# Reordering the first loads of a linear-attention and GeGLU kernel: key weights moved between two DMA queues, keys of a third tile filled in

## The chip, the cores and the metric

One core of one Trainium2 chip. The metric is the device time of one execution, in microseconds; smaller is better. The span in the profile runs from the first to the last instruction, about 1.3 us less than that time.

In the profile lines PE is TensorE, DVE VectorE, ACT ScalarE, and SPq SyncE issuing loads. L341 is line 341 of the kernel, the plain loads; L353 are the transposing loads, L453 and L454 key products, L468 and L469 query products, L539 (L541 in the changed kernel) joint products. A line of a timeline gives start, duration, engine, line and shape; the bracket at its end is the idle time before it and what ended it.

## The reference, cut to what matters

With x of 2048 x 640 in bf16, the result is `g * a + (1 - g) * b`: a linear-attention block `a` (32 heads of 20), a gated feed-forward block `b`, and a gate `g` per row.

```python
def _A_ref(x, wqkv, wo):
    qkv = (x @ wqkv) ...                     # q, k, v
    phi = lambda t: jnp.where(t > 0, t + 1, jnp.exp(t)) + 1e-6
    pq, pk = phi(q), phi(k)
    kv, z = pk^T v, sum(pk)
    return (pq kv / pq z) @ wo               # (per head; written short)

x = A_x
g = sigmoid((x * gate_w).sum(-1))
b = (gelu(x @ w_gate) * (x @ w_up)) @ w_down
```

The change touches only the start: the products of the first four row tiles of x with the key and the query weights.

## The kernel before: the parts concerned

The 640 rows of the key weights `wk` and of the query weights `wq` are cut into five chunks of 128; "wk 2" is chunk 2. A tile is 128 rows of x. Tile 0 is loaded plainly and transposed on TensorE; tiles 1 to 15 are transposed by the DMA. Each load has its own semaphore. "sp" is SyncE's queue, "act" ScalarE's.

```python
load_x(0)
load_wk(0)
load_xT(1)
load_wk(3)
load_wk(4)
load_wk(1, "act")
load_wk(2, "act")
...                                   # gate_w on "act"
for i in range(2, NQ):                # NQ = 4
    load_xT(i)
for k in range(KC):                   # KC = 5
    load_wq(k)
for i in range(NQ, NT):
    load_xT(i)
```

`KM(n, ks)` multiplies chunks `ks` of the keys of tile n (512 and 128 columns, two matmuls a chunk), `QM` the queries (the 129th column is the gate). The products of a tile with the keys, or with the queries, are one job. Job n uses two of the eight PSUM banks (where TensorE puts its results), `slot(n) = SLOTS[n % 4]`, so a query of tile 0 waits until ScalarE and VectorE (`phi1`, `phi2`) have read the keys of tile 0, and so on.

```python
for k in range(3):
    KM(0, [k])
for k in range(3):
    KM(1, [k])
KM(0, [3])
KM(1, [3])
gate_col()
KM(0, [4])
KM(1, [4])
for n in range(2 * NQ):
    if n in (2, 3):
        KM(n, ALLK)
    if n == NQ:
        for k in ALLK:
            QM(NQ, [k])               # tile 0 and tile 1 alternate
            QM(NQ + 1, [k])
    if n > NQ + 1:
        QM(n, ALLK)
    phi1(n)
    phi2(n)
for i in range(NQ, NT):
    KQ(i)                             # keys and queries of a tile together
```

Of the kernel before, what the change touches and what calls it, by code (L numbers as in the profile page):

```python
# [24 lines left out]
NQ = 4  # L25
# [137 lines left out]
def bass_gated_mix__linear_attn_block__geglu_ffn__prompt_kernel(  # L163
# [63 lines left out]
    with (  # L227
# [8 lines left out]
        with contextlib.ExitStack() as stack:  # L236
# [12 lines left out]
            def new_dma_key():  # L249
                k = "in%d" % dma_next[0]  # L250
                dma_next[0] += 1
                return k
# [16 lines left out]
            wk = wkq[:, :, 0:640]  # L269
# [38 lines left out]
            r_xT = [P.sb("xT%d" % i, R_XT, R_XT + KC * S) for i in range(NT)]  # L308
            r_xTa = [P.sb("xTa%d" % i, R_XT, R_XT + S) for i in range(NXN)]
            r_wk = [P.sb("wk%d" % k, R_WK + k * WW, R_WK + k * WW + 640) for k in range(KC)]  # L310
# [29 lines left out]
            def dma_in(dst, src, writes, reads=(), eng="sp"):  # L340
                P.op(eng, lambda e, dst=dst, src=src: e.dma_start(dst, src),  # L341
                     reads=reads, writes=writes, dma=new_dma_key())
# [3 lines left out]
            def load_x(i, eng="sp"):  # L346
                dma_in(x_aug[:, i, 0:640], A_x[0, i * 128:(i + 1) * 128, :], [r_xn[i]], eng=eng)

            def load_wk(k, eng="sp", after=()):
                dma_in(wk[:, k, :], A_wqkv[k * 128:(k + 1) * 128, 640:1280], [r_wk[k]], reads=after, eng=eng)  # L350

            def load_xT(i, after=()):
                P.op("sp", lambda e: e.dma_start_transpose(xT[:, :, i * 128:(i + 1) * 128],  # L353
                                                           A_x[0, i * 128:(i + 1) * 128, :]),
                     reads=list(after), writes=[r_xT[i]], dma=new_dma_key())

            def load_wq(k, eng="sp"):
                dma_in(wq[:, k, 0:640], A_wqkv[k * 128:(k + 1) * 128, 0:640], [r_wq[k]], eng=eng)
# [3 lines left out]
                 writes=[P.res("touch")], dma=new_dma_key())  # L362
            load_x(0)
            load_wk(0)
            load_xT(1)
            load_wk(3)
            load_wk(4)
            load_wk(1, "act")
            load_wk(2, "act")

            zero = nc.const_aps.tensor(0.0, (128, 1), F32)
            P.op("act", lambda e: e.activation(eg[:, 0:1], zero, ACT.Exp), writes=[r_eg[0]])
            P.op("dve", lambda e: e.memset(gw_sb, 0.0), writes=[r_gw])
            dma_in(gw_sb[0:5, :], gate_w.rearrange("(k p) -> k p", p=128), [r_gw], eng="act")
            for i in range(2, NQ):
                load_xT(i)
            for k in range(KC):
                load_wq(k)
            for i in range(NQ, NT):
                load_xT(i)  # L380
# [7 lines left out]
            for c in range(NHC):  # L388
# [9 lines left out]
                 reads=[r_ones], writes=[r_ident])  # L398
# [16 lines left out]
            def warm(count, n):  # L415
                def fn(e):
                    last = None
                    for w in range(count):
                        last = e.matmul(ps[:, 4, 0:n], one_l, one_r[:, 0:n], start=True, stop=True)
                    return last  # L420
                P.op("pe", fn, writes=[bank[4]])
# [4 lines left out]
            def slot(n):  # L426
                return SLOTS[n % 4]
# [17 lines left out]
            def KM(n, ks):  # L445
                i = seq[n][1]
                b0, b1 = slot(n)

                def fn(e):
                    last = None  # L450
                    for k in ks:
                        lhs = xT[:, k, i * 128:(i + 1) * 128]
                        e.matmul(ps[:, b0, :], lhs, wk[:, k, 0:512], start=(k == 0), stop=(k == KC - 1))  # L453
                        last = e.matmul(ps[:, b1, 0:128], lhs, wk[:, k, 512:640],  # L454
                                        start=(k == 0), stop=(k == KC - 1))
                    return last
                P.op("pe", fn, reads=[r_xTa[i] if i < NXN and ks == [0] else r_xT[i]] + [r_wk[k] for k in ks],
                     writes=[bank[b0], bank[b1]])

            def QM(n, ks):  # L460
                i = seq[n][1]
                b0, b1 = slot(n)

                def fn(e):
                    last = None
                    for k in ks:
                        lhs = xT[:, k, i * 128:(i + 1) * 128]
                        e.matmul(ps[:, b0, :], lhs, wq[:, k, 0:512], start=(k == 0), stop=(k == KC - 1))  # L468
                        last = e.matmul(ps[:, b1, 0:129], lhs, wq[:, k, 512:641],  # L469
                                        start=(k == 0), stop=(k == KC - 1))  # L470
                    return last
                P.op("pe", fn, reads=[r_xT[i], r_gcol] + [r_wq[k] for k in ks],
                     writes=[bank[b0], bank[b1]])

            def phi1(n):
                b0, b1 = slot(n)
                m = n % 4
                P.op("act", lambda e: e.activation(e_buf[m], ps_flat[:, b0 * 512:b0 * 512 + 640], ACT.Exp),
                     reads=[bank[b0], bank[b1]], writes=[r_e[m]])
                kind, i = seq[n]  # L480
                if kind == "q":
                    P.op("act", lambda e: e.activation(eg[:, i:i + 1], ps[:, b1, 128:129], ACT.Tanh, scale=0.5),
                         reads=[bank[b1]], writes=[r_eg[i]])

            def phi2(n):
                b0, b1 = slot(n)
                m = n % 4
                P.op("dve", lambda e: e.tensor_scalar(e_buf[m], e_buf[m], 1.0, EPS, ALU.min, ALU.add),
                     reads=[r_e[m]], writes=[r_e[m]])
                kind, i = seq[n]  # L490
                dst, r_dst = (pk[i], r_pk[i]) if kind == "k" else (pq[i], r_pq[i])
                P.op("dve", lambda e: e.scalar_tensor_tensor(
                    dst, ps_flat[:, b0 * 512:b0 * 512 + 640], 1.0 + EPS, e_buf[m], ALU.add, ALU.max),
                    reads=[bank[b0], bank[b1], r_e[m]], writes=[r_dst])

            def gate_col():

                P.op("pe", lambda e: e.matmul(ps[:, 7, 0:5], gw_sb, ident[:, 0:5], start=True, stop=True),
                     reads=[r_gw, r_ident], writes=[bank[7]])
                P.op("dve", lambda e: e.tensor_copy(wq[:, :, 640:641], ps[:, 7, 0:5].unsqueeze(2)),  # L500
                     reads=[bank[7]], writes=[r_gcol])
# [4 lines left out]
            T(0, [0], 7)  # L506
            T(0, [1, 2, 3, 4], 6)
            warm(2, 128)
            for k in range(3):
                KM(0, [k])  # L510
            for k in range(3):
                KM(1, [k])
            KM(0, [3])
            KM(1, [3])
            gate_col()
            KM(0, [4])
            KM(1, [4])
            ALLK = list(range(KC))
            for n in range(2 * NQ):
                if n in (2, 3):  # L520
                    KM(n, ALLK)
                if n == NQ:
                    for k in ALLK:
                        QM(NQ, [k])
                        QM(NQ + 1, [k])
                if n > NQ + 1:
                    QM(n, ALLK)
                phi1(n)
                phi2(n)
# [36 lines left out]
            for i in range(NQ, NT):  # L566
                KQ(i)
                if i == 4:
                    late_constants()
            P.op("dve", lambda e: e.tensor_scalar(gg, eg, 0.5, 0.5, ALU.mult, ALU.add),  # L570
                 reads=r_eg, writes=[r_g])
            P.op("dve", lambda e: e.tensor_scalar(omg, eg, -0.5, 0.5, ALU.mult, ALU.add),
                 reads=r_eg, writes=[r_omg])
# [7 lines left out]
                 reads=[r_omg], writes=[r_od], dma=new_dma_key())  # L581
# [44 lines left out]
            def ME(g):  # L626
# [6 lines left out]
                for c in cs:  # L633
# [8 lines left out]
                 reads=r_pk[0:2], writes=[r_tmp[0]])  # L642
            for i in range(2, NT):
                P.op("dve", lambda e, i=i: e.tensor_tensor(zacc, zacc, pk[i], ALU.add),  # L644
                     reads=[r_tmp[0], r_pk[i]], writes=[r_tmp[0]])
# [283 lines left out]
```

## Time and profile before

| | before |
|---|---|
| time, median of 6 runs | 273.81 us (273.72 to 274.07) |
| span | 272.6 us, PE busy 98% |
| first key product | 4.45 us |
| keys of tile 2 | 8.12 us, PE waited 0.58 us for its transpose |
| first query | 10.85 us |
| first joint product (first matmul of `KQ`) | 16.30 us |

The lines behind the table are in the prediction. The last row is the yardstick of this document. From the first joint product on PE works without a stop worth naming, and the device time less that moment is 257.6 to 257.7 us in all profiled kernels here (273.97 - 16.30 = 257.67 before). So whatever this change does shows up in that one moment.

### The profile page before, as it was taken

Reading aid. Unit: us, or ns where it says so; the run is one execution under the profiler, and the core shown is the slowest. Engines: PE = TensorE matmul, PEld = TensorE weight load, DVE = VectorE, ACT = ScalarE, POOL = GpSimd, SP = SyncE. Lnnn points to the kernel's source line nnn. Section 1 sums busy time; section 2 is a strip of 40 time slices with the busy share of each in tenths; the row PEclk is TensorE's granted clock in tenths of the full one; section 3 lists DMA queues with packets and bytes.
Section 4 is the critical chain, followed back from the end, with each engine's and each line's share of the span. In section 5 each row is a group of like instructions: output and inputs, shape, how many; then the busy total and the mean of one; then the engine's idle time right before and its main releaser. Section 6 shows DMA issues by size and latency. Waiting matters only on the chain.

```text
span 272.6 us, 3416 instructions
## 1 busy us (share of the span) xinstructions
PE 267.6 (98%) x1341; PEld 127.9 (47%) x1367; DVE 140.8 (52%) x247; ACT 75.9 (28%) x132; POOL 30.0 (11%) x28
## 2 busy tenths in 40 slices
PE   8999999999999999999999999999999999999997
PEld 3555555544445454444444444444444444444444
DVE  1678989997233335999999999634210000000200
ACT  2455555210422453232222233224011122121021
POOL 5000000003240002242332422000000000000000
DMA  7976999600200011514121221273031110110211
GB/s 192 202 115 127 346 399 388 140 2 19 58 19 2 23 50 51 192 34 49 26 48 25 49 48 27 60 219 105 5 77 38 41 38 19 38 41 19 58 58 41
DMA packets 42864, 23.78 MB, mean 87 GB/s; under 512 B 32223, under 2 KB 41439, under 8 KB 42719
## 3 DMA queue, kind: packets, MB, share of 16 engines
q1 hardware_dynamic: 42517, 23.22, 31.9%
q10 hardware_dynamic: 330, 0.33, 0.3%
q8 instruction: 11, 0.18, 0.3%
q14 instruction: 6, 0.05, 0.1%
HBM read 13.83 MB, written 2.63 MB: 60 GB/s over the span
## 4 chain that ended last, share of the span: by engine, by line
PE 96%; DMA 1%; SPq 1%; issue 1%; DVE 0%
PE ps L700 41%; PE ps L864 23%; PE ps L539 12%; PE ps L596 6%; PE ps L843 4%; PE ps L468 2%; PE ps L811 2%; PE ps L678 2%; PE ps L599 1%; DMA pool<-in_A_x_dram 1%; PE ps L453 1%; PE ps L824 1%; SPq L341 1%; PE ps L721 1%; SPq L353 0%
## 5 line engine op out<-in xcount | busy, mean ns | idle before, releaser
L700 PE MATMUL ps<-pool 128*128 128x512 bf16 x510 | 113.0, 379 | 0.5
L700 PEld LDWEIGHTS ps<-pool 128*128 128x128 bf16 x520 | 50.5, 98 | 60.0
L864 PE MATMUL ps<-pool 128*128 128x512 bf16 (+2 forms) x300 | 62.4, 366 | 0.3
L706 ACT ACTIVATE pool<-ps 128x512 f32<-128x512 f32 x52 | 31.0, 597 | 73.1 <-PE ps L700 73.1
L708 DVE TENSOR_TENSOR pool<-ps,pool 128x512 bf16<-128x512 f32 x52 | 34.7, 689 | 31.7 <-PE ps L700 30.4
L864 PEld LDWEIGHTS ps<-pool 128*128 128x128 bf16 x306 | 29.2, 98 | 33.4 <-issue 0.4
L847 DVE TENSOR_TENSOR pool<-ps,pool 128x512 bf16<-128x512 f32 x4 | 2.8, 690 | 61.5 <-PE ps L843 61.5
L539 PE MATMUL ps<-pool 128*128 128x512 bf16 (+1 forms) x176 | 32.5, 343 | 0.2
L754 POOL TENSOR_TENSOR pool<-pool 128x640 f32<-128x640 bf16 x16 | 22.4, 1404 | 73.0 <-DVE pool L756 65.6
L871 ACT ACTIVATE pool<-ps,pool 128x512 bf16<-128x512 f32 (+1 forms) x16 | 10.9, 680 | 68.6 <-PE ps L864 68.6
L539 PEld LDWEIGHTS ps<-pool 128*128 128x128 bf16 x180 | 17.6, 98 | 15.0
L558 DVE SCALAR_TENSOR_TENSOR pool<-ps,pool 128x128 bf16<-128x128 f32 (+2 forms) x36 | 21.7, 602 | 2.1
L549 ACT ACTIVATE pool<-ps 128x640 bf16<-128x640 f32 x24 | 16.9, 703 | 15.8 <-DVE pool L558 9.3
L596 PE MATMUL ps<-pool 128*128 128x512 bf16 x76 | 19.2, 379 | 0.1
L764 DVE TENSOR_TENSOR pool<-pool 128x640 bf16<-128x640 bf16 x16 | 13.2, 826 | 0.6
L762 DVE TENSOR_SCALAR pool<-pool 128x32 f32<-128x32 f32 x16 | 12.8, 802 | 0.6
L756 DVE TENSOR_REDUCE pool<-pool 128x32 f32<-128x640 f32 x16 | 12.9, 808 | 0.0
L644 DVE TENSOR_TENSOR pool<-pool 128x640 f32<-128x640 f32 x14 | 11.6, 826 | 0.5
L843 PE MATMUL ps<-pool 128*128 128x512 bf16 x51 | 11.5, 379 | 0.1
L646 POOL PARTITION_ALL_REDUCE pool<-pool x1 | 4.0, 3971 | 61.0 <-DVE pool L644 61.0
L596 PEld LDWEIGHTS ps<-pool 128*128 128x128 bf16 x78 | 7.0, 98 | 7.3
L555 DVE TENSOR_SCALAR pool<-pool 128x640 bf16<-128x640 bf16 x24 | 7.9, 327 | 1.7 <-ACT pool L549 0.4
(70 smaller groups left out, 124.1 us busy)
## 6 DMA issues: line engine op xcount, KB each, us to landing
out_dram<-pool SPq DMA_DIRECT2D x19, 128.0 KB, 1.7
pool<-in_B_w_gate_dram SPq DMA_DIRECT2D x1, 2080.0 KB, 14.8
pool<-in_B_w_up_dram SPq DMA_DIRECT2D x1, 2080.0 KB, 18.0
pool<-in_A_wqkv_dram SPq DMA_DIRECT2D x8, 160.0 KB, 3.1
pool<-in_A_x_dram SPq DMA_DIRECT2D x1, 1280.0 KB, 9.2
pool<-in_A_x_dram SPq DMA_DIRECT2D x1, 1120.0 KB, 6.3
pool<-in_B_w_down_dram SPq DMA_DIRECT2D x1, 1120.0 KB, 6.4
pool<-omg_row SPq DMA_DIRECT2D x1, 1024.0 KB, 4.8
```

What stands on the lines that cost most here:

```text
L539: last = e.matmul(ps[:, b + p, 0:c1 - c0], xT[:, k, i * 128:(i + 1) * 128], wkq[:, k, c0:c1], start=(k == 0), stop=(k == KC - 1))
L549: P.op("act", lambda e: e.activation(e_buf[m], ps_flat[:, o:o + 640], ACT.Exp), reads=banks, writes=[r_e[m]])
L558: P.op("dve", lambda e, c0=c0, c1=c1: e.scalar_tensor_tensor(dst[:, c0:c1], ps_flat[:, o + c0:o + c1], 1.0 + EPS, e_buf[m][:, c0:c1], ALU. ...
L596: last = e.matmul(ps[:, b, :], pk[i][:, c * 128:(c + 1) * 128], x_aug[:, i, 0:512], start=(i == 0), stop=(i == NT - 1))
L700: last = e.matmul(ps[:, b, :], w[:, k, fc * 128:(fc + 1) * 128], xT[:, k, j * 512:(j + 1) * 512], start=(k == 0), stop=(k == KC - 1))
L706: P.op("act", lambda e: e.activation(ge[n], ps[:, gb, :], ACT.Gelu_apprx_tanh), reads=[bank[gb]], writes=[r_ge[n]])
L708: P.op("dve", lambda e: e.tensor_tensor(hT[fc][:, j * 512:(j + 1) * 512], ps[:, ub, :], ge[n], ALU.mult), reads=[bank[ub], r_ge[n]], write ...
L754: P.op("pool", lambda e: e.tensor_tensor(tmp[n], pq[i], z_b, ALU.mult), reads=[r_pq[i], r_zb], writes=[r_tmp[n]])
L756: P.op("dve", lambda e: e.tensor_reduce(den[n], tmp[n].rearrange("p (h d) -> p h d", h=32), AX.X, ALU.add), reads=[r_tmp[n]], writes=[r_de ...
L764: P.op("dve", lambda e: e.tensor_tensor(pq[i].rearrange("p (h d) -> p h d", h=32), pq[i].rearrange("p (h d) -> p h d", h=32), den[n].unsqu ...
L843: last = e.matmul(ps[:, b, :], wd[:, fc, 512:640], hT[fc][:, j * 512:(j + 1) * 512], start=False, stop=(fc == NFC - 2), skip_group_check=True)
L864: last = e.matmul(ps[:, pb, 0:c1 - c0], lhs, rhs, start=False, stop=(q == len(rows) - 1), skip_group_check=True)
```

## The change

The intent: tile 2 had to wait for its transpose behind five key-weight loads, so one of them (wk 4) is put behind it; tile 2's keys run on the chunks at hand until wk 4 comes. Of the key weights only wk 1 is left on ScalarE's queue. The queries of tiles 0 and 1 no longer alternate. Unused parameters were dropped (cut here).

```diff
             load_xT(1)
+            load_wk(2)
             load_wk(3)
+            load_xT(2)
             load_wk(4)
+            load_xT(3)
             load_wk(1, "act")
-            load_wk(2, "act")
 ...
-            for i in range(2, NQ):
-                load_xT(i)
 ...
-            for k in range(3):
+            for k in range(2):
                 KM(0, [k])
-            for k in range(3):
+            for k in range(2):
                 KM(1, [k])
-            KM(0, [3])
-            KM(1, [3])
+            for k in (2, 3):
+                KM(0, [k])
+                KM(1, [k])
             gate_col()
+            KM(2, [0, 1])
             KM(0, [4])
             KM(1, [4])
+            KM(2, [2, 3, 4])
 ...
-                if n in (2, 3):
+                if n == NQ - 1:
                     KM(n, ALLK)
                 if n == NQ:
                     for k in ALLK:
-                        QM(NQ, [k])
-                        QM(NQ + 1, [k])
-                if n > NQ + 1:
+                        QM(n, [k])
+                if n > NQ:
                     QM(n, ALLK)
```

More of the change, by code (lines that the diff above doesn't have):

```diff
@@ L347, in load_x, with load_wk, load_xT @@
                 dma_in(x_aug[:, i, 0:640], A_x[0, i * 128:(i + 1) * 128, :], [r_xn[i]], eng=eng)
-            def load_wk(k, eng="sp", after=()):
-                dma_in(wk[:, k, :], A_wqkv[k * 128:(k + 1) * 128, 640:1280], [r_wk[k]], reads=after, eng=eng)
-            def load_xT(i, after=()):
+            def load_wk(k, eng="sp"):
+                dma_in(wk[:, k, :], A_wqkv[k * 128:(k + 1) * 128, 640:1280], [r_wk[k]], eng=eng)
+            def load_xT(i):
                 P.op("sp", lambda e: e.dma_start_transpose(xT[:, :, i * 128:(i + 1) * 128],
                                                            A_x[0, i * 128:(i + 1) * 128, :]),
-                     reads=list(after), writes=[r_xT[i]], dma=new_dma_key())
+                     writes=[r_xT[i]], dma=new_dma_key())
             def load_wq(k, eng="sp"):
```

## The prediction

> **What bounds the kernel now.** I read the page first (busy times, slices, chain), then the chain in order of time, then the PE timeline of the first 17 us, and last each transfer's time from issue to landing.
>
> ```profile
> span 272.6 us, 3416 instructions
> PE 267.6 (98%) x1341; PEld 127.9 (47%) x1367; DVE 140.8 (52%) x247; ACT 75.9 (28%) x132; POOL 30.0 (11%) x28
> PE   8999999999999999999999999999999999999997
> PE 96%; DMA 1%; SPq 1%; issue 1%; DVE 0%
> ```
>
> PE is busy for 267.6 of 272.6 us, so all idle time of PE together is 5.0 us, 1.8% of the span. The change adds and removes no arithmetic: PE, DVE and ACT have the same number of instructions in both kernels (199 and 192 merged rows each on PE and DVE when the programs are compared). It only reorders loads and matmuls of the first 14 us. Even a perfect reordering could not reach 2%. The chain shows what is at stake:
>
> ```profile
> 0.79 0.41 SPq L341
> 1.26 0.41 SPq L341
> 1.71 1.30 SPq L353
> 3.06 0.57 SPq L341
> 3.67 0.43 SPq L341
> 4.14 3.93 DMA pool<-in_A_x_dram
> 8.12 0.39 PE ps L453
> ```
>
> SyncE issues x tile 0, wk 0, transposed x tile 1, wk 3, wk 4 and then the transposed x tile 2, at 4.14 us. It lands 3.93 us later, at 8.07, and the keys of tile 2 start at 8.12. From there PE works without a break worth naming. On PE:
>
> ```profile
> 7.49 0.22 PE L454 MATMUL ps<-pool 128*128 128x128 bf16 x1
> 8.12 0.39 PE L453 MATMUL ps<-pool 128*128 128x512 bf16 x1 [0.42 <-DMA pool<-in_A_x_dram]
> ...
> 10.85 0.38 PE L468 MATMUL ps<-pool 128*128 128x512 bf16 x1
> ...
> 16.30 2.87 PE L539 MATMUL ps<-pool 128*128 128x512 bf16 x14
> ```
>
> One chunk of a key or query product (a 512 and a 128 or 129 column matmul) starts every 0.27 us (7.00, 7.27, 8.12, 8.40, 8.68 in the timeline). Without the wait, tile 2 would have started at 7.27 + 0.27 = 7.54, so this wait costs 0.58 us. It is the only large stop after the first key at 4.45. Keys of tiles 2 and 3 are 10 chunks, 8.12 + 2.72 = 10.84, and the queries start at 10.85. The four query tiles take 20 chunks, 5.45 us, to 16.30.
>
> **What the Trainium skill says.** "DMA: Bandwidth & Descriptors", section "Queues, rings and completion order": on each DMA engine one queue's descriptors are taken in ring order. The trace agrees: the loads of SyncE land in the order of issue, 2.98, 4.31, 5.53, 6.37, 6.83, 8.07, 8.77 us. Same page, section "Issuing engines are not separate DMA queues": loads from ScalarE and SyncE share the 16 engines, and a second issuer saves only issue time. The trace agrees: wk 1 and wk 2, issued by ScalarE at 1.24 and 1.71, land at 4.50 and 4.88, between SyncE's wk 0 and x tile 1, with the engines' busy share at 0.90 from 2 to 4 us and 1.08 from 4 to 6. "TensorE: Matmul & The Clock Gate", section "Part 1: The HAM clock gate" says that idle time throttles the clock only after some 3.4 us; no wait here is near that, and the granted clock is 1.00 in every stretch.
>
> **The change part by part.**
>
> 1. wk 2 leaves ScalarE. Of the loads ahead of x tile 1 one is gone. wk 2's data moved from about 4.3 to 4.8 us, beside x tile 1's, so x tile 1 should land some 0.3 us earlier, at about 5.2. That matters, because the keys of tile 1 now come after two chunks of tile 0, at 5.34 (after 4.45 and 4.93) where before it was 5.61.
>
> 2. On SyncE, wk 2 and wk 3 take the places of wk 3 and wk 4: issues at 3.06 and 3.67. With the queue drained 0.35 us earlier I put them at 6.37 - 0.4 = 6.0 and 6.83 - 0.4 = 6.45. PE has four chunks done at 5.34 + 2 x 0.27 = 5.88, so it waits for wk 2 until about 6.05: a new wait of 0.15 us. Chunks 2 and 3 of both tiles then run to 6.05 + 4 x 0.27 = 7.15.
>
> 3. x tile 2 keeps its issue at 4.14, but one load of 160 KB fewer lies ahead of it. Those took 0.4 to 0.5 us each in the saturated stretch (the landings 6.37 and 6.83). And in the trace 13 of its 16 completions come only at 7.93 to 8.07, half a microsecond after the first three (7.36 to 7.45), while x tile 3's transpose, right behind it, is streaming; x tiles 1 and 3, followed by plain loads, show no such split. Now wk 4 follows. So 8.07 - 0.45 = 7.6 if the split stays and about 7.1 if it goes; I take 7.15. Its first two chunks then fill 7.2 to 7.75.
>
> 4. wk 4 is now issued behind x tile 2, at 5.40 instead of 3.67. Loads of this size took 2.7 to 3.3 us from issue to landing, and the first wq, also issued behind a transpose, took 2.7: 5.40 + 2.65 = 8.05. PE waits 0.3 us more, then runs chunk 4 of tiles 0 and 1 (0.54), three chunks of tile 2 (0.81) and tile 3 (1.36): 8.1 + 2.71 = 10.8. Tile 3's transpose, issued at 5.87 and landing about 8.8, is in time for 9.45. So the queries start at about 10.8 against 10.85: a gain of 0.05. The old 0.58 us wait is mostly cut into smaller ones (wk 2, wk 4).
>
> 5. Five wq loads come after that, one issue later: 7.2 to 9.2 instead of 6.72 to 8.76. Before:
>
> ```profile
> 6.72 2.48 SPq L341 DMA_DIRECT2D pool<-in_A_wqkv_dram  x5
> 9.24 16.34 SPq L353 DMA_TRANSPOSE pool<-in_A_x_dram  x12
> ```
>
> They landed at 9.40, 10.13, 10.55, 11.54 and 12.05. The total of bytes ahead of them is unchanged, so where the engines set the pace they land as before; where the issue does, 0.47 later. The queries of tiles 0 and 1 no longer alternate. Alternating, chunk k was due at 10.85 + 0.54k, the last at 13.0, a microsecond after wq 4. Now the last chunk of tile 0 is due at 10.8 + 4 x 0.27 = 11.9, and wq 4 lands at 12.05 to 12.5. With 12.2 the wait is 0.3 to 0.35 us. Alternation had to go, though: the keys of tile 1 finish 1.05 us later than before, so the VectorE pass that frees their PSUM banks ends at about 10.48 + 1.05 = 11.5, too late for an alternating query of tile 1 at 11.1 but in time for 12.1 or later.
>
> Sum: -0.05 at the start of the queries, +0.3 in them: +0.25 us by the middle estimates. All later work is PE after PE in the chain, so it arrives at the end unchanged. If wq 4 keeps its 12.05, and the split of x tile 2's completions goes, it is about +0.1. I cannot tell the landings to better than 0.3 us, and a change that lowers two known waits deserves some credit; I choose +0.05, that is 273.76 + 0.05 = 273.8.
>
> **The rivals.**
>
> - *The wait simply goes.* x tile 2 lands by 7.15, wk 4 by 7.75, wq 4 before 11.6. Then PE runs from 6.05 without a stop: 6.05 + 15 chunks x 0.272 + 0.05 = 10.2, and 0.6 us is won: 273.1. For it: the queue is shorter in front of both. Against it: wk 4's issue alone is 1.73 us later, and it would have to land in 2.35 us, which only the first, unhindered load managed (2.19).
> - *The loads behind take over.* wq 3 and wq 4 shift by the full issue of 0.47 (wq 4 at 12.5): the last chunk of tile 0 starts at 12.55 and tile 1's queries end at 12.55 + 6 x 0.272 = 14.2, against 13.57 before: 274.4. For it: about 1.6 us lay between issue and first packet for the first wq, so issue may set the pace. Against it: the engines are nearly always busy here (0.92 share from 10 to 12, 1.07 from 12 to 14).
> - *Nothing at the end.* Some later stop in the key and query stage that depends on a load or on VectorE (88% busy there) absorbs the shift. Against it: from 16.30 on PE has idle pieces below 0.1 us only. Time: 273.8.
>
> **Range and chances.** The rivals give 273.1 to 274.4; runs of the kernel before spread over 0.35 us. I set 273.2 to 274.4. A 2% change is 5.5 us, more than the whole idle time of PE, so either side beyond 2% has half a per cent, for a state that I do not foresee.
>
> **What would show it right or wrong.** In the changed profile: the first key of tile 2 by 7.2 to 7.7 rather than 8.12 (step 3); a PE wait for the key weights of some 0.15 us near 6 (step 2) and one of about 0.3 near 8 (step 4); the first query near 10.8; a wait for the query weights near 11.5 to 12.2 that the kernel before does not have (step 5); the first product of keys and queries together at 16.3 to 16.6 instead of 16.30. The prediction is wrong if that last time is before 15.8 or after 16.9, or if the distance from it to the end (256.3 us) changes by more than 0.3.

## The result, and the profile after

The changed kernel took 274.78 us (median of 6 runs, 274.72 to 275.06) against 273.81: 0.97 us slower, outside the predicted range. The ratio is 1.0035, with a 95% interval of 1.0022 to 1.0048. Ratios here are the mean time of one kernel's fast runs over that of the other's of the same rounds, so not quite the ratio of the medians that are quoted.

The page of the changed kernel, for comparison with the first lines in the prediction (before: 272.6 us, PE 98%):

```profile
span 273.4 us, 3442 instructions
PE 270.0 (99%) x1367; PEld 128.3 (47%) x1367; DVE 140.7 (51%) x247; ACT 76.0 (28%) x132; POOL 30.0 (11%) x28
PE 95%; SPq 3%; DMA 1%; issue 0%; DVE 0%
```

PE is busier and the kernel slower: busy time says nothing about the loss. (The 26 matmuls more are records missing from the trace of before; both programs have the same number, and a later trace of the kernel before has 1367 too.) The third line, the chain by engine, gives it away: SyncE's queue has grown from 1% to 3% of the path. The chain in order of time:

```profile
4.17 1.21 SPq L353
5.42 0.57 SPq L341
6.04 1.21 SPq L353
7.29 0.57 SPq L341
7.91 0.43 SPq L341
8.38 0.43 SPq L341
8.86 0.43 SPq L341
9.33 3.31 DMA pool<-in_A_wqkv_dram
12.68 0.39 PE ps L468
```

Before, the chain left the queue at 4.14 us with tile 2's transpose. Now it stays on SyncE's queue through wk 4 (5.42), tile 3 (6.04) and all five query weights, until the last, wq 4, is issued at 9.33 and lands 3.31 us later. Only then PE takes over. The PE timeline shows two of the three waits that the prediction announced, and the yardstick. (The third, for wk 2 near 6 us, did not come: PE was still slow then, of which below, and asked for wk 2 at 6.44, after it had landed at 6.22.)

```profile
8.14 0.22 PE L454 MATMUL ps<-pool 128*128 128x128 bf16 x1
8.55 0.39 PE L453 MATMUL ps<-pool 128*128 128x512 bf16 x1 [0.19 <-DMA pool<-in_A_wqkv_dram]
...
12.31 0.22 PE L469 MATMUL ps<-pool 128*128 128x129 bf16 x1
12.68 0.39 PE L468 MATMUL ps<-pool 128*128 128x512 bf16 x1 [0.15 <-DMA pool<-in_A_wqkv_dram]
...
17.05 1.24 PE L541 MATMUL ps<-pool 128*128 128x512 bf16 x5
```

Matmuls overlap, so a wait is read from the starts. The chunk after 7.92 was due at 8.19 and started at 8.55: 0.36 us for wk 4. The queries started at 11.28 (10.85 before). The last chunk of tile 0 was due at 12.36 and started at 12.68: 0.32 us for wq 4. After that the distance to the joint product is the same as before. So 0.43 + 0.32 = 0.75 us later at 17.05, which is what the profiled executions differ by (274.74 against 273.97: 0.77); the medians differ by 0.97.

SyncE's timeline shows the issues behind it, first before, then changed:

```profile
4.14 2.53 SPq L353 DMA_TRANSPOSE pool<-in_A_x_dram  x2
```

```profile
4.17 1.21 SPq L353 DMA_TRANSPOSE pool<-in_A_x_dram  x1
5.42 0.57 SPq L341 DMA_DIRECT2D pool<-in_A_wqkv_dram  x1
6.04 1.21 SPq L353 DMA_TRANSPOSE pool<-in_A_x_dram  x1
7.29 2.47 SPq L341 DMA_DIRECT2D pool<-in_A_wqkv_dram  x5
9.81 16.17 SPq L353 DMA_TRANSPOSE pool<-in_A_x_dram  x12
```

A plain load takes 0.43 us of SyncE's time, but 0.57 right behind a transpose (also in the chain above: 7.29 against 7.91). The change adds one such switch: every query weight is issued 0.57 us later (7.29 to 9.33 instead of 6.72 to 8.76).

### The profile page after: what moved, and what is told of

It is laid out like the page before. It is cut to its first block, busy times and chain, and to the rows that moved or that the text cites. A ratio compares the mean times of both kernels' runs of the same rounds, so it can differ in the third digit from the quotient of the medians.

```text
span 273.4 us, 3442 instructions
## 1 busy us (share of the span) xinstructions
PE 270.0 (99%) x1367; PEld 128.3 (47%) x1367; DVE 140.7 (51%) x247; ACT 76.0 (28%) x132; POOL 30.0 (11%) x28
## 4 chain that ended last, share of the span: by engine, by line
PE 95%; SPq 3%; DMA 1%; issue 0%; DVE 0%
PE ps L702 41%; PE ps L866 23%; PE ps L541 12%; PE ps L598 6%; PE ps L845 4%; PE ps L813 2%; PE ps L680 2%; SPq L341 2%; PE ps L601 1%; SPq L353 1%; PE ps L468 1%; DMA pool<-in_A_wqkv_dram 1%; PE ps L826 1%; PE ps L723 1%; PE ps L741 0%; PE ps L469 0%
## 5 line engine op out<-in xcount | busy, mean ns | idle before, releaser
L551 ACT ACTIVATE pool<-ps 128x640 bf16<-128x640 f32 x24 | 16.9, 704 | 15.8 <-DVE pool L560 9.3
```

Of the source, the lines that this page charges most:

```text
L551: P.op("act", lambda e: e.activation(e_buf[m], ps_flat[:, o:o + 640], ACT.Exp), reads=banks, writes=[r_e[m]])
```

## The experiments

There were eighteen experiments: thirteen new kernels, one of them twice, the kernel before three times more and the changed one once more. "FJP" is the start of the first joint product in a run's profile (before 16.30, changed 17.05); landings are read from the completion counts in the trace (each load counts 16 completions, and the last is its landing). All runs were correct, except the two that were made wrong. Times are medians of 5 or 6 runs, or of one where a kernel was run for its profile alone; the kernel before had medians of 273.78 to 274.20 in the rounds they shared. In the first two of the five sets of experiments measured together (these two were on one chip, the others each on another), 7 of its 21 fast runs took 275.0 to 275.9 us, which widens those intervals; the reason is taken up below. One more run of it, at 355.59 us, is slow and was left out.

### Each half of the change alone

The loads of the change with the matmul order of before:

```diff
-            for k in range(2): KM(0, [k])   ...   (matmul order of the change)
+            for k in range(3): KM(0, [k])   ...   (matmul order of before, alternating queries)
```

> Loads issued as in the changed kernel, matmuls in the order of the kernel before (alternating queries too). Theory 'place in the queue' (each landing follows its issue by about 3.1 us, and the load behind the transpose is what costs): wk 2 lands at 6.2, wk 4 at 8.5; PE waits for wk 2 after two chunks and for wk 4 at 8.55; chunk 4 of tiles 0 and 1, then tiles 2 and 3, first query at 8.55 + 12 x 0.272 = 11.8, no wait for wq with alternation, first joint product at 17.3 (16.30 before, 17.05 changed): 274.8, as slow as the changed kernel or 0.2 slower. Rival 'clock' (the four key chunks at 0.53 us instead of 0.27 in the changed kernel are the loss): here the slow chunks fall into the wait for wk 2, so most of the loss goes: first joint product by 16.7, 274.2. Rival 'order' (the matmul order costs, not the loads): as before, 273.8.

Measured: 275.56 us (274.93 to 276.18), ratio 1.0043 (1.0010 to 1.0075). In the profiled run (274.93): wk 2 landed at 6.10, wk 4 at 8.56, wq 4 at 12.80; PE waited at 6.14 and 8.60, FJP 17.34. The loads alone cost what the place in the queue says; the rivals' 16.7 and 16.3 are out (a repeat, below, had 17.01). The spread of the times was not expected.

The matmul order of the change with the loads of before:

```diff
-            load_wk(2) / load_xT(2) ahead of load_wk(4) / load_xT(3)
+            load_wk(3), load_wk(4), load_xT(2), load_xT(3); load_wk(2, "act")
```

> Loads issued as in the kernel before, matmuls in the order of the changed one. Place in the queue: x tile 2 lands at 8.07 with most of its completions late, since tile 3's transpose is behind it again; all of chunks 0 to 3 is done by 7.6, PE waits to 8.12 and has 12 chunks left instead of 10: first query at 11.4; wq 4 at 12.05 is in time for 12.5; first joint product at 16.8: 274.3. Clock: slow chunks before 6.4 are hidden by the wait at 8.12 and make no difference. Order alone as the cause: 274.7, as the changed kernel.

Measured: 274.44 us, ratio 1.0002 (0.9969 to 1.0034; the interval is wide, as two runs of before at 275.9 fell into it; all five runs, 274.22 to 274.62, lie above its eight shorter ones, 273.65 to 274.18). In the profile tile 2 landed at 8.19 and FJP was 16.95, 0.15 later than expected. So each half alone is slower in the profile (17.34 and 16.95 against 16.30), and their losses do not add up: both together are at 17.05. These are single profiles. With the repeats the loads alone have 17.34 and 17.01 and the changed kernel 17.05 and 17.36, so by the profiles the new loads alone cost as much as the whole change; that the new order wins a part back is not shown.

### The order of the queries

```diff
-                        QM(n, [k])                       # changed
+                        QM(NQ, [k]); QM(NQ + 1, [k])     # alternate again
```

> The changed kernel with the queries of tiles 0 and 1 alternating chunk by chunk again. Place in the queue: no wait for wq 4 any more (0.32 us won), but the first query of tile 1 is due at 11.55 and its PSUM banks come free when VectorE ends at 12.04: a wait of 0.54 us takes its place; first joint product at 17.25 against 17.05, 275.0. If the alternation was dropped for nothing, it is 16.75 and 274.45.

Measured: 274.75 us, FJP 17.09. The wait moved, as expected: the PE timeline shows it now for VectorE (the banks) instead of the DMA.

```profile
11.90 0.39 PE L468 MATMUL ps<-pool 128*128 128x512 bf16 x1 [0.39 <-DVE pool L492]
```

That chunk was due at 11.34, so it cost 0.56 us. wk 4 happened to land at 8.30, 0.2 earlier than in the changed kernel, which is why the sum is level. Dropping the alternation was not the mistake: keeping it is no better.

```diff
-                        QM(n, [k])                                     # all of tile 0, then tile 1
+       # chunks 0-3 of tile 0, chunks 0-3 of tile 1, then chunk 4 of both
```

> The changed kernel with the queries in the order: chunks 0 to 3 of tile 0, chunks 0 to 3 of tile 1, then chunk 4 of both. Place in the queue: both the wait for wq 4 (due at 13.45 instead of 12.37, lands 12.64) and the wait for tile 1's banks (due 12.37, free 12.04) are gone; 0.32 us won: first joint product at 16.73, 274.45. If wq 4's lateness is not what costs there, no change: 274.75.

Measured: 274.58 us, FJP 16.90. No wait is left after the first query, which started at 11.45 (wk 4 landed at 8.67): 11.45 + 5.45 = 16.90. That is 0.15 us under the changed kernel although wk 4 landed 0.17 later, in sum the 0.3 us expected for wq 4. The median, 0.2 under those of the changed kernel and of the alternating one, points the same way.

### Taking the waits away

Here chunk 4 of the first key tiles is multiplied by wk 3, so that it needs no wk 4. Its output is wrong, which doesn't matter for the time.

```diff
-  e.matmul(ps[:, b0, :], lhs, wk[:, k, 0:512], ...)            reads r_wk[k]
+  e.matmul(ps[:, b0, :], lhs, wk[:, min(k, 3), 0:512], ...)    reads r_wk[min(k, 3)]
```

> The changed kernel with chunk 4 of the keys multiplied by wk 3 (wrong result on purpose), so that the first four key tiles do not wait for wk 4. Theory 'two waits in a row' (wk 4 and wq 4 both hold PE up, and the later one covers the earlier): chunk 4 starts at 8.2, the keys of tile 3 end near 10.95 instead of 11.28, and PE then waits the longer for wq 4 (12.6 to 12.8): first joint product at the landing of wq 4 plus 4.4, 17.0 to 17.2, as in the changed kernel, 274.7 to 274.9. Rival 'wk 4 is the loss': the 0.36 us comes off, 16.7, 274.4.

Measured: 274.89 us (the changed kernel in the same rounds 274.97), FJP 17.47. Queries started at 10.98, 0.3 earlier than in the changed kernel, and nothing came of it:

```profile
12.42 0.22 PE L469 MATMUL ps<-pool 128*128 128x129 bf16 x1
13.10 0.39 PE L468 MATMUL ps<-pool 128*128 128x512 bf16 x1 [0.46 <-DMA pool<-in_A_wqkv_dram]
```

wq 4 landed at 13.05, and 13.05 + 4.4 is the 17.47. The wait for wk 4 is covered by the one for wq 4.

With the last query chunk freed in the same way too:

> As the one before, and chunk 4 of the queries multiplied by wq 3 (wrong on purpose too). Two waits in a row: both waits gone, PE is held up at most by wq 3 (11.9 to 12.4, due 11.75): first joint product at 16.6 to 17.0, 274.3 to 274.6; the rest of the loss against 16.30 is then wq 3. Rival 'something else' (clock, PSUM): still 17.05 and 274.8.

Measured: 274.76 us, FJP 17.40, later than expected. Now PE waits for wq 3, one load earlier in the queue (landed 12.71):

```profile
12.76 0.39 PE L468 MATMUL ps<-pool 128*128 128x512 bf16 x1 [0.56 <-DMA pool<-in_A_wqkv_dram]
```

Over the six runs the mean is only 0.27 us below that of the changed kernel in the same rounds. So in these profiles the changed kernel is not held by one wait but by a stream: the query weights as a whole come too late for queries that take them at one chunk per 0.27 us.

The changed kernel itself once more, in these rounds:

> The changed kernel itself in the rounds of these experiments. wk 4 lands at 8.2 to 8.7, wq 4 at 12.6 to 12.8, first joint product at 17.0 to 17.2, 274.7 to 275.0. Since PE waits for wk 4 until 8.3 to 8.7 anyway, a half rate that ends by 7 us costs nothing; only one that lasts to 8 would show.

Measured: 274.97 us (274.78 to 275.16), ratio 1.0033 (1.0018 to 1.0048); wk 4 at 8.53, wq 4 at 12.94, FJP 17.36, 0.16 later than the window given. Here too PE waited first for wq 3 (landed 12.52, chunk started 12.56) and then for wq 4.

### Why the query weights are late: issue or traffic

This is the kernel before with one load of 128 bytes more, which brings SyncE's extra switch without the traffic:

```diff
             load_xT(2)
+            tiny()          # plain load, 16 x 4 elements
             load_xT(3)
```

> The kernel before with one plain load of 128 bytes on SyncE's queue between the transposes of tiles 2 and 3: one more switch from a transpose to a plain load, as the change has, and no traffic to speak of. Theory 'issue' (SyncE's issue times set the landings behind): tile 3 and all wq loads are issued 0.57 later and land later by about that, wq 4 near 12.9 (12.05 to 12.5 in the four profiles of before). Rival 'traffic' (bytes set them): wq 4 stays at 12.05 to 12.5. On tile 2, theory 'successor': followed by a plain load it lands at 7.3 to 7.7 instead of 7.9 to 8.65. If so, tile 2's keys start at 7.55, tile 3's wait for its transpose until about 9.25, queries at 10.6, first joint product near 16.1: 273.7, at best 0.2 better than before.

SyncE's timeline of that kernel:

```profile
4.15 1.21 SPq L353 DMA_TRANSPOSE pool<-in_A_x_dram  x1
5.40 0.57 SPq L364 DMA_DIRECT2D pool<-in_A_wqkv_dram  x1
6.01 1.20 SPq L353 DMA_TRANSPOSE pool<-in_A_x_dram  x1
7.26 2.48 SPq L341 DMA_DIRECT2D pool<-in_A_wqkv_dram  x5
```

128 bytes take the same 0.57 us of SyncE as the 160 KB of wk 4, the query weights are issued from 7.26 on, and wq 4 landed at 12.86, 12.75 in the next run. In six profiles with the loads of before (the kernel before four times, the one with only the matmul order changed, and one with more matmuls ahead of the first key) it was 12.05 to 12.50, mean 12.32; in nine with the loads of the change 12.56 to 13.12, mean 12.82. So the issue alone gives the whole shift of half a microsecond; the traffic of a key load is not needed for it. (The two runs with the small load were on another chip than the later profiles of the loads of before. On each of the two chips that ran both orders of loads, the landings were 0.3 to 0.8 apart.)

The same two runs bear on tile 2's landing. With a plain load behind its transpose it landed at 7.54 and 7.51, as in the changed kernel (7.31 to 7.96, mean 7.55, in nine profiles), though as many loads lay ahead of it as before. With another transpose right behind it, it took until 7.88 to 8.65 (mean 8.21, six profiles). The change got its 0.66 us there from what comes behind tile 2, not from the load taken from in front of it. Whether it is the plain load itself, or that the next transpose is issued 0.6 us later for it (6.01 against 5.40), these runs do not separate.

The time was 274.02 us, one of six runs at 275.57 (the profiled one, FJP 17.89, of which below); ratio 1.0019 (1.0002 to 1.0035). It is no improvement.

Whether a plain load ahead of a transpose also lands late, as a pattern in the completion counts suggested, was tried by the same small load in two other places of the changed kernel:

```diff
             for k in range(KC): load_wq(k)
+            tiny()                              # first kernel: ahead of tile 4's transpose
 ...
             load_wk(4)
+            tiny()                              # second kernel: ahead of tile 3's transpose
```

> The changed kernel with one plain load of 128 bytes put on SyncE's queue between wq 4 and the transpose of tile 4. Theory 'successor' (the load just ahead of a transpose in the queue gets 11 to 13 of its 16 completions half a microsecond or more late; in the changed kernel wk 4 and wq 4 are such loads): wq 4's late completions (11.69, then 12.56 to 12.64) go, it lands at about 11.8, the last query chunk of tile 0 (due 12.37) waits for nothing, first joint product at 16.73 instead of 17.05, 274.45. Rival 'traffic' (the engines are just busy there): wq 4 at 12.6, no change, 274.8.

Measured: 274.78 us, FJP 17.25; wq 4 at 12.83 and the tiny load behind it at 13.09, both with the late completions. The theory fails here.

> The changed kernel with the same small load between wk 4 and the transpose of tile 3. Successor: wk 4's completions all come near 7.85 instead of half of them at 8.4 to 8.5, so the wait of 0.36 us at 8.55 goes (chunk 4 at 8.19). Tile 3's transpose is then issued some 0.45 later and lands near 9.75, 0.2 after it is due, and wq 4 lands near 13.1, due 12.3: in sum no gain, first joint product near 17.5, 275.2. Traffic: wk 4 at 8.5 as before, and all that follows 0.45 later.

Measured: 275.26 us, FJP 17.53; wk 4 at 8.12, against 8.22 to 8.98 in the nine other profiles with its load in that place. A shift of that size is inconclusive. What sets wk 4's landing beyond its issue stays open.

### Moving loads to ScalarE's queue

```diff
-            load_wk(4)                                  # on SyncE's queue
+            load_wk(4, "act", after=[r_wk[1]])          # on ScalarE's, once wk 1 is there
-            KM(2, [0, 1]); KM(0, [4]); KM(1, [4]); KM(2, [2, 3, 4])
+            KM(0, [4]); KM(1, [4]); KM(2, ALLK)
```

> The changed kernel with wk 4 taken off SyncE's queue: ScalarE issues it once wk 1 has landed (4.5 us), and chunk 4 of tiles 0 and 1 goes ahead of tile 2. Place in the queue: wk 4 lands by 7.6 instead of 8.2 to 8.7, and all wq loads are issued 0.57 earlier, at 6.72 to 8.76 as in the kernel before, and land as there (wq 4 12.05 to 12.3 instead of 12.6 to 12.8). Tile 2 is again followed by a transpose and lands near 8.1, just as chunk 4 ends (8.25). First query near 10.95 (11.28 changed, 10.85 before), wq 4 due 12.05: wait 0 to 0.3; first joint product at 16.4 to 16.7, 273.9 to 274.2, most of the loss given back. Rival 'traffic' (the engines, not the issue, set the landings): wq 4 still at 12.6 to 12.8, first joint product at 16.95 or later, 274.7.

Measured: 275.60 us, ratio 1.0055 (1.0043 to 1.0067), FJP 18.17: the highest median of all, and a clear miss of both theories. wk 4, issued at 4.52, landed at 9.40, and tile 2's transpose, issued at 4.21, at 9.58. The DMA issues of that kernel, transpose and load, in us to landing:

```profile
pool<-in_A_wqkv_dram ACTq DMA_DIRECT2D x1, 160.0 KB, 4.9
pool<-in_A_x_dram SPq DMA_TRANSPOSE x1, 5.4
```

The same loads in one queue took 2.8 to 3.6 and 3.1 to 4.5 us. The query weights, issued at 6.79 to 8.84 as before the change, did land as before it (wq 4 at 12.23), as the issue theory has it; PE was held by wk 4 long before that.

```diff
+            load_wq(3, "act", after=[r_wk[3]]); load_wq(4, "act")     # wk 1, wk 2 on "act" too
+            SyncE: x 0, wk 0, xT 1, wk 3, xT 2, wk 4, xT 3, wq 0 to 2
+            KM(2, [0, 1, 2, 3]); KM(0..2, [4])
```

> Try for a faster version: wk 1 and 2 on ScalarE's queue as in the kernel before; on SyncE's x tile 1, wk 3, x tile 2, wk 4, x tile 3, wq 0 to 2; wq 3 and 4 on ScalarE's queue once wk 3 has landed. Keys: chunks 0 to 3 of tiles 0 and 1, chunks 0 to 3 of tile 2, then chunk 4 of all three, then tile 3. Place in the queue with successor: wk 3 at 6.4, x tile 2 at 7.0, wk 4 near 8.05, x tile 3 at 8.9 to 9.2; PE works through from 6.97 with waits of 0.3 us at most, first query at 10.3 to 10.6, wq 3 and 4 at 9.5 to 10 and so in time: first joint product at 15.75 to 16.05 (16.30 before), 273.2 to 273.5. If the engines' traffic sets the pace, the two wq push tile 3 to 9.6 and later: 273.8 or more.

Measured: 275.06 us, FJP 17.45. The keys went as hoped (PE was ready for the first query at 10.55; before 10.85), but wq 3, issued by ScalarE at 6.52, landed at 10.11, wq 0, issued by SyncE at 6.80, only at 11.47, and PE waited until 11.60. Again loads took longer while two queues were at work: 4.6 to 4.9 us for wq 0, 1, 2 and 4. That the sharing is the reason is argued, not shown; in the kernel before, wk 1 and wk 2 on ScalarE's queue beside tile 1's transpose took 3.2 to 3.3 us, and the transpose 3.8.

### The half rate of the first key chunks

In the changed kernel's profile the first four key chunks take some 0.53 us each, 4.35 to 6.44, and all later ones 0.27. In the kernel before only the first two were slow. So a rival was at hand from the start: TensorE's clock. "TensorE: Matmul & The Clock Gate" in the Trainium skill, "Part 1: The HAM clock gate", says that TensorE runs at half rate until it has been busy for some 3.4 us, that the window is free-running, and that the same kernel therefore differs from run to run. To see such runs, the kernel before and one of the above were profiled again.

> The same kernel as the one with the loads of the change and the matmul order of before, whose six times spread from 274.93 to 276.18, only the fastest with a profile. If the PE clock is the reason (PE idles for 1.1 us waiting for wk 2 at 5 us, and the half rate of the first chunks goes on after it), a profile of a slow execution shows key chunks at 0.53 us after 6.2 and the first joint product later than 17.34 by just what the time is above 274.93, with the loads landing as before. If the loads are the reason, wk 4 or wq land later and the chunks are at 0.27. If it is as fast as the first, nothing is learnt of it.

Measured: 274.69 us, FJP 17.01; nothing learnt of the longer runs, as said.

> The kernel before itself, for a profile. In the two earlier calls 7 of its 21 fast runs took 275.0 to 275.9, the others 273.6 to 274.2; no profile of such a run is at hand. Rival 'clock': a run of the longer kind shows key chunks at 0.53 us until after 7.5, tile 2 starting at 9.5 or later instead of 8.12, loads landing as usual. Rival 'loads': chunks at 0.27, and a load landing 1.5 us late. Rival 'elsewhere': the first joint product at 16.3 and the time lost after it.

Measured: 275.13 us, FJP 17.46, a run of the longer kind. The PE timeline (loads as usual, tile 2 landed at 8.31):

```profile
4.71 0.58 PE L453 MATMUL ps<-pool 128*128 128x512 bf16 x1 [0.59 <-DMA pool<-in_A_wqkv_dram]
5.19 0.63 PE L453 MATMUL ps<-pool 128*128 128x512 bf16 x1
...
7.33 0.63 PE L453 MATMUL ps<-pool 128*128 128x512 bf16 x1
7.86 0.63 PE L453 MATMUL ps<-pool 128*128 128x512 bf16 x1
8.39 0.42 PE L453 MATMUL ps<-pool 128*128 128x512 bf16 x1
...
9.27 0.38 PE L453 MATMUL ps<-pool 128*128 128x512 bf16 x1
```

Seven chunks at half rate, until 8.39; the keys of tile 2 start at 9.27, with no wait for a load. The two further draws:

> The same kernel once more, for another draw; same expectations.

> The same kernel once more, for another draw; same expectations.

Measured: 273.78 us (FJP 16.11, half rate gone by 4.5) and 274.54 us (FJP 16.88; half rate until 6.9, tile 2 landed at 8.65). With the first profile's 5.3, the half rate of one and the same kernel ended at 4.4, 5.3, 6.9 and 8.4 us; in the run of 275.57 us above (the same matmuls) it went on to 9.3. The stretches of the longer run, PE's busy time second and the granted clock after the busy times:

```profile
4.71:8.39 3.68, 3.68 (x14) 1.73 (x15) 0.00 (x0) 0.00 (x0) 0.00 (x0) 1.00 1.04 208
9.27:10.90 1.63, 1.63 (x14) 0.92 (x13) 0.93 (x2) 1.30 (x3) 0.00 (x0) 1.00 0.89 256
```

Seven key chunks take 3.68 us and then six take 1.63 (the x14 of the second stretch counts matmuls that only overlap its edges too), so 0.53 and 0.27 us a chunk, and the granted clock is given as 1.00 in both: this record does not show the half rate, the distance of the starts does. What is hidden under the wait for tile 2 costs nothing; the rest is lost. In the changed kernel PE waits for wk 4 until 8.55 in any case: at full rate, with wk 2 at 6.22, its six chunks up to there would have run from 6.27 to about 7.95 instead of 8.19, into that same wait. So its half rate cost nothing, and the clock is not the cause of its loss. A profile says the same: in the kernel that does not wait for wk 4 the chunks ran at full rate from the first on (4.37, 4.64), and FJP was 17.47.

Would a shorter gap ahead of the first key help?

```diff
-            warm(2, 128)
+            warm(5, 128)          # three short matmuls more, in the kernel before
```

> The kernel before with 5 instead of 2 short matmuls in the gap between the transposes of tile 0 and its first key (PE idle for 0.3 to 0.7 us there). If that gap is why the half rate of the first key chunks sometimes lasts until 8.4 us (a run of before at 275.13), no run is above 274.5. If the end of the half rate comes at a time of its own, the spread stays: about one run in four above 274.9. The median should be that of before, 273.7 to 274.1, either way.

Measured: 273.92 us, six runs from 273.82 to 274.03, ratio 0.9994 (0.9980 to 1.0009); in the profile all key chunks ran at full rate. With the small load as well:

> The same with the gap ahead of the first key filled by 5 short matmuls instead of 2, as in the earlier run that had all six times between 273.82 and 274.03. If both hold, this is the best version: 273.5 to 273.8 with no run above 274.5. If filling the gap did nothing and that earlier run was luck, one or two of the six are above 274.5.

Measured: 273.84 us (273.78 to 274.41), ratio 1.0007 (0.9994 to 1.0020), FJP 16.25. None of these 11 runs was above 274.5, but of the kernel before's 22 runs in the same rounds only one was (275.17). That the gap matters is not shown, and no version was found that beats the kernel before.

## Why the prediction was wrong, point by point

- **The bound was right.** PE bounds the kernel, the change acts on the first 17 us only and stays far below 2%, and everything after is moved unchanged (256.35 us from the first joint product to the end, 256.3 before). The prediction's own sign of being wrong, a first joint product after 16.9, came: 17.05.
- **Steps 1 to 3 held in their landings, one for another reason.** Tile 1 landed at 5.04 (5.2 said), wk 2 at 6.22 (6.0), tile 2 at 7.31 (7.15). The 0.15 us wait for wk 2 in step 2 did not come. Its sum had only the first two chunks at half rate; four were. Tile 2's gain came from the plain load behind it; the case for "one load fewer ahead" fell with the kernel that had them all ahead and landed at 7.54.
- **Step 4 had wk 4 too early.** It took 2.65 us from issue to landing as the term, the best value in the view; it was 3.08, and 2.8 to 3.6 over nine profiles. wk 4 landed at 8.50, not 8.05, and the queries started at 11.28, not 10.8: +0.43 us in the prediction's sum where it had -0.05. But the run without that wait was as slow as the changed kernel, so this error did not decide the end. It would have been the next limit: the run without a wait for the query weights still had 16.90, not 16.30.
- **Step 5 is the one that failed, by size.** "With 12.2 the wait is 0.3 to 0.35 us": the mechanism was right, the landing was 12.64 in the profile and 12.82 on average. The wait itself came out at 0.32, but by luck: the chunk was due 0.46 later than said (12.36, not 11.9) and wq 4 landed 0.44 later than said. With 12.64 the step's own sum gives 12.68 + 0.27 + 1.36 + 2.73 = 17.04 for the first joint product, which is what was measured, whatever the keys did. Two things went into the mis-sizing. The 12.05 it started from was one draw, the earliest of six (mean 12.32). And it left open whether issue or traffic sets these landings, and put the shift at 0.15 us, where it is the full issue delay: 0.50 us between the two means. It also put that delay at 0.47, without the 0.57 us of a plain load behind a transpose, though the chain of before, quoted in the prediction, shows that number (3.06 0.57).
- **The credit of 0.2 us was a choice without a number behind it.** The working came to +0.25 and was rounded down to +0.05. The rival "The loads behind take over" (274.4, with wq 4 at 12.5) was the one that came true.
- **A miscount in a rival.** "The wait simply goes" counts 15 chunks from 6.05 on. Of 20 key chunks four are done by then, so it is 16: 10.45 instead of 10.2, and 0.4 us won instead of 0.6. It did not decide anything, as that rival did not come.
- **A check that told nothing.** The prediction read the granted clock of 1.00 as showing full rate. The chunks of 0.53 us stood under that same 1.00; in the profile of before the first two were there to be seen.

What stays open: no run gave the changed kernel its query weights at the old times with all else the same (the one that tried was held by wk 4); why wk 4 took 2.8 to 3.6 us; why two queues at once took 4.9 and 5.4 us; and whether filling the gap shortens the half rate. Of the runs of before of 275 us and more, only one has a profile; that the others have the same cause is argued, not shown. The same holds for the spread of the kernel with only the loads changed.

## What to carry to other kernels

When a load moves between queues, work out the issue time of everything behind it on that queue, since a small or early load delays a later, unrelated stream; here 128 bytes moved the query weights by half a microsecond. Two waits in a row need not be a sum: look at the later one first, because it can cover the other, as here. And a landing time from one profile is one draw; use its range, above all where the slack is of the same size.

## What the Trainium skill lacked or had wrong

- "DMA: Bandwidth & Descriptors", "Issuing engines are not separate DMA queues", has the issue time "usually small relative to the DMA itself". Here it was 0.43 us for a plain load, 0.57 behind a transpose and 1.2 to 1.3 for a transpose, against landings of some 3 us, and it set the landings of the query weights: 0.57 us more of issue with 128 bytes of traffic moved wq 4 from a mean of 12.32 to 12.75 and 12.86.
- The same section says that loads of both queues share the engines and interleave. That two queues at once can cost much is missing: a load on ScalarE's queue beside a transpose on SyncE's took 4.9 and 5.4 us to land, against 2.8 to 3.6 and 3.1 to 4.5 without that. Why is not shown here.
- No page says that a DMA transpose's completion depends on what follows it in the queue: it landed at 7.88 to 8.65 us with a transpose behind it and at 7.31 to 7.96 with a plain load, issued at 4.14 to 4.21 in all of these (the run with two queues in use at once left out).
- "TensorE: Matmul & The Clock Gate", "Part 1: The HAM clock gate", is right that the end of the half rate differs from run to run, but gives ±500 ns for it (and, for another kernel, 6 to 14 slow matmuls). Profiles have it anywhere up to 9.3 us, in some before the first key at 4.4, with PE first busy at 0.82 and idle for 0.3 to 0.7 us ahead of the first key; the runs at 8.4 and 9.3 took 275.13 and 275.57 us, where most others of the same kernels took 273.6 to 274.4.
